# Two attention patterns and a soft mixture of experts: output stationaries read with a step, inputs packed in full tiles, another order

## The chip, the cores and the metric

The kernel runs on one core of one Trainium2 chip. Its time is device microseconds of one execution. Before the change three runs took 154.91 us at the median (154.8 to 155.06). The profile is of one further execution, which took 154.55 us.

## The reference, cut to what matters

```python
B, H, S, D = 4, 8, 768, 64                   # q, k, v: float32; is_retrieval = [1,0,1,0,0,0,1,0]
scores = q @ k.T / 8                         # for each batch and head
keep = causal & (retrieval[h] | (pos_k < 4) | (pos_q - pos_k < 64))
a = softmax(where(keep, scores, -1e9)); x = (a @ v) as (B*S, H*D) = (3072, 512)

logits = x @ phi                             # (3072, 32): 8 experts of 4 slots
d = exp(logits - max over tokens); d /= its sum over tokens
slot_in = d.T @ x                            # (32, 512)
slot_out[e] = relu(slot_in[e] @ w1[e]) @ w2[e]      # w1 (8,512,1024), w2 (8,1024,512)
c = softmax(logits over the 32 slots)
out = c @ slot_out                           # (3072, 512) float32
```

Every token of every batch takes part in the softmax over tokens, so nothing of the experts can start before the attention of the last batch has ended, and nothing of the output before the last expert.

## The kernel before, in words

**The order is written out.** The kernel builds its work as named operations (`Plan.op`), each with the engine it runs on, the operations it depends on, and the buffers it takes and gives back. The long string `ORDER` then says in which order they are emitted; `/A`, `/D` and `/P` put an operation on ACT, DVE or POOL. Each engine runs its own part of that string in order. A dependency becomes a wait in the engine's instruction stream, so what stands behind a waiting operation on the same engine waits too. SP issues the ten output stores, the flags and phi; POOL issues all other loads, since they turn float32 into bf16 on the way.

**Loading.** `slots` are twelve 8 KB-per-partition buffers. The twelve q, k and v loads (`Lq0` to `Lv3`, 768 KB in bf16 each, 96 partitions of 2 x 2048 elements) and the first twelve weight loads (`Lw0` to `Lw11`, 1 MB each) go through them. `Lw12` to `Lw15` go into memory that the attention has finished with: `Lw15` into the last batch's q and k (deps `qks[3]`). `Lw0` to `Lw7` are w1, `Lw8` to `Lw15` w2. The order of loads is Lq0 Lk0 Lv0 Lw0 Lq1 Lk1 Lv1 Lw1 Lw2 Lq2 Lk2 Lv2 Lw3 Lw4 Lw5 Lq3 Lk3 Lv3 Lw6 and so on.

**Attention.** A raw tensor is transposed on PE in four groups of 16 (`Tq0.0`, line 387: 64 columns of the raw tile at a time, 96 rows), into one PSUM bank (`TR`, two of them); each group is copied out by one instruction of 768 columns (`Eq0.0`, lines 232 and 234). For v a second transposition follows (`V2.p`, line 438, with `VB.p`). A pair p = 4b + n holds the heads n and n + 4 of batch b. For each pair there are five score groups `QK.p.0` to `QK.p.4` (line 406) into the PSUM buffers `SC` (two), their exponentials `EX.p.g` on ACT (line 474, 128x1024 each), their masks `MK.p.g` on DVE (line 418), six sums `PV.p.i` (line 522) into `PV` (one), the division `NM.p` on DVE (lines 533 and 535), and a transposition `XT.p` with its copy `XE.p` (line 547). `VF.p` (line 454) multiplies v with the head flags, mostly on POOL. `QX.b` and `EXX.b` do one score block of each pair of a batch together.

**Slots.** For each batch `LG.b` (line 561) makes the logits of its 768 tokens four times over, on 128 partitions, `EL.b` their exponentials `eTs` (128 partitions x 768 tokens), `DS.b` (line 618) the weighted sums of tokens, and `SA.b` adds them up. For the last batch these are `LGa.3`, `LTa`, `LTb`, `LGb.3`, `ET`, `DS.3`, `SA.3`, `EL.3`.

**The end.** After `SA.3`: `SI` and `SIE` bring the slot inputs into place (lines 673, 677), `H.e4.c` is the hidden layer of four experts, half c (line 687, 16 products each), `HR` its relu (lines 697, 699), `TH` and `HE` transpose it (line 708), `W2.e` the second layer of expert e (line 742), the last in two halves `W2.7.0` and `W2.7.1`, `SO` the scaling of the result (lines 757, 759). For the output, `EE.b` rearranges `eTs` into `expT` so that a stationary of 128 tokens is contiguous; `RW` (line 724) multiplies each of the 24 stationaries with a column for the softmax denominators, and `RWR` takes the reciprocals. The outputs are 24 products `OMf0` to `OMf23` (line 767), with their scaled copies `OEf` to SBUF (lines 772 and 774, on ACT and DVE) and ten stores `STf` (line 802). Product m = 4 gi + r makes the rows 512 gi + 4 p + r for the 128 partitions p, so a store of four r writes 8 KB in one run for each partition.

**Zeros.** `fill` puts products with zeros (line 330, `Z..`) on PE, each 128x512. `Z5`, eight of them, is a dependency of `W2.7`; `Z0`, `Z1` to `Z4` stand ahead of operations in the same way. The fills `Z60` to `Z67` depend on an early transposition only, and nothing depends on them.

The functions that the diff touches and what calls them, with the profile's line numbers:

## Time and profile before

| what | us |
|---|---|
| median of three runs | 154.91 |
| the profiled execution | 154.55 |
| its span, first to last instruction | 152.7 |
| PE busy | 133.0 |
| DVE busy | 113.4 |
| ACT busy | 107.5 |
| POOL busy | 33.5 |

The span lacks 1.85 us of the execution's own time. Times within the profile are counted from the span's start. A busy PE is not a PE at its peak: the products are pipelined, and a wait inside a stretch does not always show. PE's weight loads have a row of their own (PEld) and overlap the products. The profile's granted clock of PE is 1.00 at full and 0.50 at half speed; it is 0.969 over the span. A line of a group shows its count after an x, then busy microseconds and the mean nanoseconds of one. Lines 232, 234 and 239 are helpers (the copies on ACT and DVE, and the loads), so their rows are told apart by their tiles.

### The profile page before, as it was taken

How to read it: one execution, taken by the hardware profiler on the slowest of the kernel's cores; microseconds unless marked ns; L12 is line 12 of the kernel's file. 1: busy time of each engine (PE TensorE's matmuls, PEld its weight loads, DVE VectorE, ACT ScalarE, POOL GpSimd, SP SyncE). 2: the span in 40 equal slices, each digit the busy share in tenths (PEclk: the TensorE clock that was granted, in tenths of full speed). 3: DMA queues.
4: the chain of work that ended last, by engine and by line, in shares of the span. 5: the costliest groups of instructions: out<-in, count | busy, mean ns of one | idle time of the engine just before them, and what ended most of it. 6: DMA issues, size and time to landing. Idle time of an engine off the chain costs nothing.

```text
span 152.7 us, 5227 instructions
## 1 busy us (share of the span) xinstructions
PE 133.0 (87%) x2313; PEld 83.1 (54%) x2313; DVE 113.4 (74%) x257; ACT 107.5 (70%) x124; POOL 33.5 (22%) x51
## 2 busy tenths in 40 slices
PE   6999799999999999999989999998999689787100
PEld 2355456676677657677656676665673348232000
DVE  3955698999978799999998998999975322166900
ACT  3023699999999999999879999999917710266300
POOL 6910005750031060505520202405110000000000
PEclk9999999999999999999999999999999959999975
DMA  2999999999999999999999999999999992059995
GB/s 34 200 215 224 213 211 211 217 219 225 201 215 213 227 210 212 225 203 216 211 229 215 212 212 223 210 215 219 219 212 215 221 204 58 4 178 411 417 423 219
DMA packets 6950, 32.91 MB, mean 215 GB/s; under 512 B 1296, under 2 KB 1296, under 8 KB 4496
## 3 DMA queue, kind: packets, MB, share of 16 engines
q0 software_dynamic: 4800, 26.22, 83.8%
q1 hardware_dynamic: 2128, 6.37, 10.7%
q8 instruction: 18, 0.29, 0.7%
q14 instruction: 4, 0.03, 0.1%
HBM read 52.50 MB, written 6.29 MB: 385 GB/s over the span
## 4 chain that ended last, share of the span: by engine, by line
PE 59%; DVE 17%; DMA 8%; ACT 5%; issue 3%; POOL 2%; DVEq 0%; POOLq 0%; ACTq 0%
PE pv L522 13%; PE sc L406 13%; PE tr L387 9%; DMA slot<-in_v_dram 8%; DVE pt L418 5%; DVE slot L774 4%; PE sc L330 4%; PE tr L547 4%; PE tr L438 3%; DVE xv L535 3%; PE pv L742 3%; PE sc L561 3%; PE sc L687 3%; ACT pt L474 2%; DVE qk L234 2%
## 5 line engine op out<-in xcount | busy, mean ns | idle before, releaser
L474 ACT ACTIVATE pt<-sc 128x1024 bf16<-128x1024 f32 x80 | 77.6, 1026 | 4.8 <-PE sc L406 3.4
L418 DVE TENSOR_TENSOR pt<-pt,msk 128x512 bf16<-128x512 bf16 (+1 forms) x80 | 37.8, 503 | 1.2 <-ACT pt L474 1.2
L406 PE MATMUL sc<-qk 64*128 64x512 bf16 (+3 forms) x256 | 32.5, 309 | 0.0
L522 PEld LDWEIGHTS <-pt 128*128 128x128 bf16 x640 | 24.7, 97 | 9.1 <-issue 6.4
L522 PE MATMUL pv<-vx,pt 128*128 128x65 bf16 x352 | 27.9, 193 | 0.9 <-DVE xv L535 0.7
L387 PE MATMUL tr<-ident,slot 96*64 96x96 bf16 x768 | 24.1, 209 | 1.7 <-DMA slot<-in_v_dram 0.9
L454 POOL TENSOR_TENSOR vf<-vx,fm 128x528 bf16<-128x528 bf16 x14 | 15.5, 1112 | 44.8 <-DVE vx L234 43.0
L387 PEld LDWEIGHTS <-slot 96*64 96x64 bf16 x768 | 18.9, 110 | 10.6 <-issue 7.7
L522 PE MATMUL pv<-vf,pt 128*128 128x65 bf16 x288 | 22.7, 195 | 0.0
L330 PE MATMUL sc<-zero 128*128 128x512 bf16 x66 | 19.5, 429 | 1.2 <-DVE zero L321 1.2
L234 DVE COPY qk<-tr 128x768 bf16<-128x768 bf16 x28 | 14.9, 550 | 4.7 <-PE tr L387 4.5
L535 DVE TENSOR_TENSOR xv<-pv,rs 128x768 bf16<-128x768 f32 x16 | 15.3, 958 | 0.6
L406 PEld LDWEIGHTS <-qk 64*128 64x128 bf16 x256 | 9.2, 94 | 7.2 <-issue 1.6
L234 DVE COPY xT<-tr 128x768 bf16<-128x768 bf16 (+1 forms) x15 | 8.6, 570 | 5.2 <-PE tr L708 4.2
L239 POOL DMA_DIRECT2D slot<-in_moe_w_dram x12 | 6.8, 569 | 22.7 <-PE tr L387 16.3
L330 PEld LDWEIGHTS <-zero 128*128 128x128 bf16 x66 | 6.2, 108 | 9.1 <-issue 4.4
L232 ACT COPY qk<-tr 128x768 bf16<-128x768 bf16 x4 | 3.2, 797 | 10.8 <-PE tr L387 10.8
L234 DVE COPY xv<-tr 128x768 bf16<-128x768 bf16 x14 | 7.6, 552 | 1.9 <-PE tr L387 1.7
L547 PE MATMUL tr<-ident,xv 128*128 128x128 bf16 x96 | 8.1, 220 | 0.0
L438 PE MATMUL tr<-ident,xv 128*128 128x128 bf16 x96 | 8.0, 220 | 0.0
L234 DVE COPY vx<-tr 128x768 bf16<-128x768 bf16 x12 | 6.4, 551 | 1.0 <-PE tr L438 1.0
L547 PEld LDWEIGHTS <-xv 128*128 128x128 bf16 x96 | 5.6, 97 | 2.1 <-issue 1.8
(102 smaller groups left out, 135.3 us busy)
## 6 DMA issues: line engine op xcount, KB each, us to landing
slot<-in_moe_w_dram POOLq DMA_DIRECT2D x12, 1024.0 KB, 25.5
slot<-in_q_dram POOLq DMA_DIRECT2D x4, 768.0 KB, 18.4
slot<-in_k_dram POOLq DMA_DIRECT2D x4, 768.0 KB, 21.4
slot<-in_v_dram POOLq DMA_DIRECT2D x4, 768.0 KB, 23.7
out_dram<-slot SPq DMA_DIRECT2D x3, 1024.0 KB, 5.6
out_dram<-slot SPq DMA_DIRECT2D x5, 512.0 KB, 3.6
qk<-in_moe_w_dram POOLq DMA_DIRECT2D x2, 1024.0 KB, 18.3
vx<-in_moe_w_dram POOLq DMA_DIRECT2D x1, 1024.0 KB, 21.5
```

What stands on the lines that cost most here:

```text
L234: nc.vector.tensor_copy(dst, src)
L239: emit=lambda o: e.dma_start(dst(), src))
L330: nc.tensor.matmul(scb[buf.slot][:, 0, :], zero[:, 0:128], zero, start=True, stop=True)
L387: nc.tensor.transpose(t[64 * i:64 * (i + 1), :, s, :], rv[:, i, 8 * c + s, :], ident[0:96, 0:96])
L406: nc.tensor.matmul(scb[sc.slot][:, i, c:c + 128 * nb], kk, qq.rearrange("p b c -> p (b c)"), start=True, stop=True)
L418: e.tensor_tensor(pT[:, :, 0:w], pT[:, :, 0:w], mh[:, :, c:c + w], op=ALU.mult)
L438: nc.tensor.transpose(t[:, 128 * j:128 * (j + 1)], vT[:, 6 * n + j, :], ident)
L454: e.tensor_tensor(vfs[VFb[p].slot], vv, mm, op=ALU.mult)
L474: nc.scalar.activation(pTs[PTb[b, n].slot][:, :, 512 * g:512 * (g + 1)], scb[sc.slot], ACT.Exp, scale=scale)
L522: nc.tensor.matmul(pvb[:, h, 65 * i:65 * (i + 1)], lt, rhs, start=(j == 0), stop=(j == i))
L535: nc.vector.tensor_tensor(xo, pvw[:, :, :, 0:64], r.rearrange("p i (j o) -> p i j o", o=1).to_broadcast([P, 2, 6, 64]), op=ALU.mult)
L547: nc.tensor.transpose(t[:, 128 * i:128 * (i + 1)], xv[:, i, 128 * n:128 * (n + 1)], ident)
```

## The change

1. **Output stationaries.** For two thirds of the output (gi 2 to 5) the stationary is read out of `eTs` itself, every sixteenth column of the first 2048 tokens; only the last 1024 tokens are still rearranged into `expT` (gi 0 and 1), by two operations, `EE.2` (a third of a batch) and `EE.3`. The rows of an output tile gi of 2 to 5 are then 16 blocks of 8 x 4 neighbouring rows, and a store's pattern in DRAM has the dimensions 16, 8 and the run.
2. **Packing.** q, k and v of the batches 1 to 3, 864 rows in all, are laid one behind another into tiles of 128 rows: seven instead of nine. A tensor that crosses from a tile into the next is loaded in two parts. A tile's group of transposes handles all its rows, and one copy for each tensor in it follows (`Ek1.0.32/D` copies the rows from 32 on).
3. **Small work.** The second half of the slot tables goes to GpSimd, and `phi` to ACT. The tables `edist`, `phf` and `ri` lie in parts of `eTs` that are filled later.
4. **Zeros.** `Z5` is gone as a dependency. Ten fills `Z70` to `Z79` of two products each may stand anywhere behind `Z4`; in the new order `Z77` stands before `RW`, `Z73`, `Z71` and `Z75` before `W2.7.0`, the rest among the outputs.
5. **Order.** The whole string is another one. q of batch 3 is loaded ahead of `Lw3`. `EE.3` and `RW` stand ahead of `H`, the four `H` stand together, both `W2.7` ahead of `SO`.

```diff
+zero Lri Lq0 warm tables ident keypos flags Tq0.3 Lk0 Tq0.1 Lv0 Z0 hm3 Eq0.3/A hm0 Eq0.1/A Tq0.2 Tq0.0 Lw0
...
+LTa LGa.3 NM.15 XT.15 XE.15/D Z1 LTb LGb.3 Z2 ET DS.3 Z3 SA.3 EL.3 SI EE.3/D Z4 Lw15 Z77 RW SIE RC RWR H.0.1
+H.0.0 HR.0.1/D H.1.0 HR.0.0/A H.1.1 HR.1.0/A TH.0 HR.1.1/A TH.1 HE.0/D W2.0 W2.1 HE.1/D W2.2 W2.3 W2.4 W2.5
+W2.6 Z73 Z71 Z75 W2.7.0 W2.7.1 SO.0/D OMf0L SO.1/A OMf0R OMf1 OMf2 OEf0L OMf3 OEf0R OMf4 OEf1/A OMf5 STf0.0
...
-    expT = xv_mem[:, 6144:9216].rearrange("p (r c) -> p r c", r=4)
+    expT = sb.tile([P, 4, 256], BF16, name="expT")
...
+    tiles = [[(x, 0, 0, 0, 96)] for x in "qkv"]
+    row = 0
+    for b_, x_ in [(b_, x_) for b_ in range(1, B) for x_ in "qkv"]:
+        r0 = 0
+        while r0 < 96:
+            if row % 128 == 0:
+                tiles.append([])
+            n_ = min(96 - r0, 128 - row % 128)
+            tiles[-1].append((x_, b_, row % 128, r0, n_))
+            row, r0 = row + n_, r0 + n_
+    tbufs = [Buf("S8") for _ in tiles]
...
+    def emit_slot_tables(o):
+        nc.gpsimd.tensor_scalar(sum4, jrow[:, 0:NS], pc[:, 3:4], None, op0=ALU.is_equal)
+        nc.gpsimd.tensor_tensor(pc[:, 4:5], pc[:, 4:5], pc[:, 5:6], op=ALU.subtract)
...
                     for i in range(2):
                         nc.tensor.transpose(t[64 * i:64 * (i + 1), :, s, :], rv[:, i, 8 * c + s, :],
-                                            ident[0:96, 0:96])
+                                            ident[0:rows, 0:rows])
...
+            for x, b, p0, r0, n in parts:
+                tb = {"q": QTb, "k": KTb, "v": VTb}[x][b]
...
+                def emit_e(o, c=c, tr=tr, p0=p0, r0=r0, n=n, dst=dst):
+                    copy(o, dst()[:, r0 // 4:(r0 + n) // 4, 32 * c:32 * (c + 1)],
+                         tr_bf(tr.slot, 8 * rows).rearrange("p (x y) -> p x y", y=32)[:, p0 // 4:(p0 + n) // 4])
...
+    def evs(x, b, n=None):
+        return [o for r0, o in ev[x, b] if n is None or r0 < 24 * n + 24]
...
-    for b in range(B):
-        eto[b] = pl.op(f"EE.{b}", "ACT DVE", deps=[elo[b], dsp] + [xto[p] for p in range(12, 16)],
-                       emit=lambda o, b=b: emit_ee(o, b))
+    for b, x0 in ((2, 4), (3, 0)):
+        def emit_ee(o, b=b, x0=x0):
+            d_ = expT[:, :, 32 * (6 * b + x0 - 16):32 * (6 * b - 10)].rearrange("p r (x t a) -> p r x t a", t=4, a=8)
+            copy(o, d_, eTs[:, b, 128 * x0:768].rearrange("p (x a r t) -> p r x t a", a=8, r=4, t=4))
...
+    for i in range(10):
+        fill(f"Z7{i}", 2, [z4])
...
+    ef = eTs.rearrange("p b (k u) -> p u (b k)", u=16)
     def out_lhs(gi, r):
-        return expT[:, r, 128 * gi:128 * (gi + 1)]
+        return expT[:, r, 128 * gi:128 * (gi + 1)] if gi < 2 else ef[:, 4 * r + gi - 2, 0:128]
+    out_v = out.rearrange("(x t a r) d -> t x a r d", t=4, a=8, r=4)
+    out_n = out.rearrange("(g p r) d -> g p r d", p=128, r=4)
+    def out_dst(gi, r, c):
+        return out_n[4 + gi, :, r, c] if gi < 2 else out_v[gi - 2, 0:16, :, r, c]
...
-                z5 = [fill("Z5", 8, w2o[-1:] + [o_rwm])]
...
-            bf = Buf(["SC", "TR", "SC", "TR", "PV"][cyc % 5])
+            bf = Buf(["TR", "SC", "TR", "SC"][cyc % 4] if u < 12 else ["SC", "TR", "SC", "TR", "PV"][cyc % 5])
...
+              emit=lambda o, x=(gi, rr, cc): nc.sync.dma_start(out_dst(*x), ot_view(x[0])[:, x[1], x[2]]))
```

More of the change, by code (lines that the diff above doesn't have):

```diff
@@ L261, in w_view, with load_w @@
         return m.rearrange("p (a f) -> p a f", a=4 if i < NE else 8)
-    def load_w(i, deps=()):
+    def load_w(i, deps=(), rows=(128,), half=None):
         if i < NE:
@@ L348 @@
             for n in range(4)}
-    o_phi = pl.op("phi", "DVE", deps=o_ph, emit=lambda o: nc.vector.tensor_copy(
+    o_phi = pl.op("phi", "ACT", deps=o_ph, emit=lambda o: nc.scalar.copy(
         phi4.rearrange("p n (g s) -> p n g s", g=4),
@@ L419, in mask_emit @@
         return f
-    for b in range(B):
-        for x in "qkv":
-            transposes(x, b)
+    for g in range(len(tiles)):
+        transposes(g)
     tq0 = [o for o in pl.ops if o.name == "Tq0.3"]
```

271 lines of the change are left out of this document (143 added, 128 removed).

## The prediction

> **What bounds the kernel now.** I read the page's forty slices first, then windows, then the chain of waits from the end backwards, then the issues by tensor. The slices (3.8 us each, DMA busy in tenths, then GB/s written):
>
> ```profile
> span 152.7 us, 5227 instructions
> ...
> DMA  2999999999999999999999999999999992059995
> GB/s 34 200 215 224 213 211 211 217 219 225 201 215 213 227 210 212 225 203 216 211 229 215 212 212 223 210 215 219 219 212 215 221 204 58 4 178 411 417 423 219
> ```
>
> There are two long stretches with every DMA engine busy, and a hole between them. The first is the loading, the second the stores. So whatever the engines do, the time is: end of the loads, plus the hole, plus the stores. The last load (the second one into qk, which is Lw15) and the ten stores, from the answers on those tiles:
>
> ```profile
> L239 POOL DMA_DIRECT2D qk<-in_moe_w_dram x1: 536/536/536, 110.7 to 110.7; - x1
> ...
> DMA to landing us min/median/max: 17.9/17.9/17.9
> ```
> ```profile
> L802 SPq DMA_DIRECT2D out_dram<-slot x10: 332/332/547, 134.7 to 145.4; - x10
> ...
> DMA to landing us min/median/max: 2.5/3.9/6.2
> ```
> ```profile
> 76.00:113.00 37.00, 35.81 (x671) 24.24 (x669) 34.69 (x75) 33.57 (x38) 8.40 (x12) 1.00 1.04 217
> 117.30:129.60 12.30, 10.31 (x216) 6.56 (x216) 4.16 (x8) 3.60 (x5) 0.00 (x0) 0.86 0.80 167
> 134.70:151.60 16.90, 5.43 (x20) 1.63 (x17) 8.73 (x13) 6.10 (x10) 0.00 (x0) 0.85 0.93 372
> ```
>
> Lw15 is issued at 110.7 and lands 17.9 later, at 128.6. The first store is issued at 134.7, the last at 145.4, and that one lands 6.2 later, at 151.6; 1.1 us more end the span. The windows (columns: stretch, length, then busy time of PE, weight loads, DVE, ACT, POOL, the granted clock, DMA share, GB/s) show the stores at 0.93 of all engines over their 16.9 us, with DVE and ACT busy for only 8.7 and 6.1 of it: **the stores set their own length**, and it starts to run at the first store. So the question is when that store leaves. From the landing of Lw15 to it lie 6.1 us. The chain of waits there (start, length, what):
>
> ```profile
> 115.84 0.70 DVE msk L634
> ...
> 116.58 0.32 PE tr L673 x4
> ...
> 116.99 0.30 DVE msk L677
> ...
> 117.34 1.94 PE sc L687 x32
> ...
> 119.30 1.27 ACT msk L697 x2
> ...
> 120.62 0.72 PE tr L708 x8
> ...
> 121.36 0.69 DVE xT L234
> 122.05 0.67 DVE msk L699
> ...
> 122.76 1.90 PE sc L687 x16
> 124.66 0.73 PE tr L724 x24
> 125.39 1.37 PE pv L742 x24
> 126.76 0.64 PE tr L708 x8
> 127.40 2.30 PE pv L742 x80
> 129.70 1.83 PE sc L330 x8
> 131.53 0.36 PE pv L742 x8
> ...
> 131.91 0.48 ACT msk L757
> ...
> 132.44 0.40 PE pv L742 x8
> ...
> 133.62 0.50 PE sc L767 x2
> ...
> 134.20 0.49 DVE slot L774
> ```
>
> Read it as: slot sums (SA.3), SI, SIE, the hidden layer H (L687), its relu HR (L697, L699), its transpose TH and copy HE, the slot weights' row sums RW (L724), W2 (L742), eight zeros Z5, the last expert W2.7, its scaling SO, the first output row. All of it is PE's order, not data: W2.7.0 needs Lw15, there at 128.6, but starts at 131.53. **The hole has 2.9 us that no transfer asks for** ahead of W2.7.0, and 3.2 us behind it.
>
> **The change part by part.** The terms move the first store; the stores' length follows.
>
> *The end of attention.* The rows for the packed transposes and evictions:
>
> ```profile
> L387 PE MATMUL tr<-ident,slot 96*64 96x96 bf16 x768 | 24.1, 209 | 1.7 <-DMA slot<-in_v_dram 0.9 <-DVE qk L234 0.5 <-DVE msk L305 0.2
> ...
> L234 DVE COPY qk<-tr 128x768 bf16<-128x768 bf16 x28 | 14.9, 550 | 4.7 <-PE tr L387 4.5
> ...
> L232 ACT COPY qk<-tr 128x768 bf16<-128x768 bf16 x4 | 3.2, 797 | 10.8 <-PE tr L387 10.8
> ...
> L234 DVE COPY elg<-tr 128x192 bf16<-128x192 bf16 x3 | 0.8, 252 | 0.2 <-PE tr L583 0.2
> ```
>
> The nine later tensors, 864 rows, become seven tiles, so 28 groups of 16 transposes replace 36. A group costs 24.1/48 = 0.50 (all 48 groups are in that row). Eight fewer save 4.0 us of PE if a group of 128 columns costs what one of 96 does, and lose 0.8 if it costs by the column (28 x 0.67 against 36 x 0.50); I take 2 saved, between them, spread over 70 us. But the evictions grow from 36 to 52: sixteen times a group is cut in two. From 550 ns for 768 columns and 252 for 192, a column costs 0.52 ns and an instruction 0.15 us, so 16 cuts cost at most 2.5 us in all; by the pace of copies that follow one another it is less, some 1.2. By the written order ACT keeps three of its nine full copies (797 ns each) inside the attention and gets two small pieces, EG.1 and phi; what it drops goes to DVE, which in turn drops phi, one VF and the second half of the slot tables. In the window 76 to 113 DVE has 34.69 of 37.00 and ACT 33.57: both are near full, DVE the fuller. After 76 us my count of the two orders gives ACT 1.4 us less (EL.1 is earlier, VB.13 goes to DVE, EG.1 comes) and DVE about nothing (three full evictions less, four small ones, VB.11 and VB.13, EE.2 more, VF.13 less). So the end of attention moves between -1.4 (ACT's share) and +0.6 (the cuts not covered); I take -0.5, since DVE is the fuller.
>
> The slot tables on GpSimd and four more load issues (split tensors; some 0.66 each, the row of the k loads below) cost nothing: POOL is busy 8.4 of 37 us, and the loads behind them are issued long before their turn (Lw15 17.9 ahead). Without that cover they would be 2.6 us and the small ops. Lw14 now stands ahead of VF.15 on POOL, and PV.15 waits for VF.15; but Lw14's last condition, DS.2, stands before QK.15 in the new order, so I cost it at nothing, and at what DS.2 is late if it slips.
>
> *From SA.3 to H.* EE.3 and RW now stand ahead of H on their engines: DVE does SA.3, EE.3, SIE, and PE does RW before H.0.1, so H waits for both. The rows, from the timeline:
>
> ```profile
> 117.20 1.69 DVE L234 COPY xv<-eT 128x768 bf16<-128x768 bf16 x2
> ...
> 120.45 1.62 ACT L232 COPY xv<-eT 128x768 bf16<-128x768 bf16 x1
> ...
> 120.61 0.57 PEld L708 LDWEIGHTS <-msk 128*128 128x128 bf16 x8 [1.00 <-ACT msk L697]
> ...
> 124.59 0.71 PEld L724 LDWEIGHTS <-xv 128*128 128x128 bf16 x24 [0.84 <-issue]
> ```
>
> EE.3 on DVE is 1.69/2 = 0.85: from 116.54 to 117.39. RW took 0.73 with 24 contiguous loads, 0.71/24 = 30 ns each. Sixteen of them now step 16 elements. No row shows that step; the transposes of L708 load with a step of 8 and take 0.57/8 = 71 ns. Bounds: nothing (RW 0.73), or double the excess of L708 (+1.3, RW 2.0). I take L708's 71 for each, the nearest row: +0.66, RW 1.39, to 118.8. So H starts at 118.8 instead of 117.34: **+1.46**. In the 24 output products the same loads are covered by the stores. The Trainium skill (SBUF — State Buffer, Door 1: The DMA port swizzle) calls steps of up to 8 bf16 elements free and lets longer ones pay at each new 16-byte line. The trace does not agree on the first, 71 ns against 30, and has no longer step; if each load reads 128 lines at either step, as the rule has it, the two cost the same, which is the 71 taken here.
>
> *H to the last W2.* Before, 12.2 us (117.34 to 129.70 less RW 0.73 is 11.6 of own work): H.1.0 waits for HR.1.1, which waits behind HE.0 on DVE, and runs at half clock (16 products 1.90, where 32 took 1.94). After, the four H stand together: 4 x 0.97 = 3.88, to 122.7. TH.0 0.64 to 123.3; meanwhile HR.1.0 and HR.1.1 on ACT, 1.27, from 122.7 to 124.1 with two hand-overs; TH.1 0.64 to 124.75; seven W2 at 2.30/5 = 0.46 each, 3.22, to 128.0. EE.2's 1.62 on ACT, and EE.0 and EE.1, are gone from here. The zeros: Z5's eight took 1.83; "no forced zeros" is only half so, since Z73, Z71 and Z75 stand at the same place, 6 x 0.23 = 1.37, to 129.35. With -0.5 from attention **W2.7.0 starts at 128.85**, against 131.53. Lw15 forbids anything before 128.6, so a faster attention brings 0.25 more and then nothing. That landing should not move by more than 1 us either way: the same bytes in almost the same order, behind a queue that the slices show full throughout.
>
> *W2.7.0 to the first store.* Before 3.18: W2.7.1 waits for SO.0, then SO.1, then two products. After, both halves run first (0.76), SO.0 on DVE and SO.1 on ACT together (0.48), two half products in one bank (0.4), the two evictions together (0.49), and some 0.17 of hand-overs: 2.3. First store at 131.15, **3.56 earlier** than 134.71.
>
> *The stores.* Same ten, same bytes, same run of one to four rows for each partition, in the same order; evictions keep their pace and their banks differ little. I take 16.9 unchanged, which is a choice: two thirds of the bytes now go to 16 blocks of 8 partitions, and no row shows that form (rival 2).
>
> Sum: profiled time 154.55 - 3.56 = 151.0. The three runs have a median 0.36 above the profiled one, so **151.3**.
>
> **The rivals.** *1, the hole closes less, for attention is late.* A tile is transposed only when both tensors in it have landed. Tq3 was ready with q3; now it needs k3, and every QK and PV stands behind it on PE (Tv1 waits for q2 in the same way):
>
> ```profile
> L239 POOL DMA_DIRECT2D slot<-in_k_dram x4: 641/663/702, 3.1 to 45.5; - x4
> ...
> DMA to landing us min/median/max: 9.0/21.4/30.8
> ```
>
> The last k lands at 45.5 + 30.8 = 76.3 and PE, in order, stands there if it comes sooner; DVE at 34.69 of 37 cannot win it back. With +1.5 instead of -0.5, W2.7.0 is at 130.85: 153.3, faster still. For it: both engines nearly full. Against: two SC buffers keep ACT fed for 2 us.
>
> *2, the stores get slower, and so the kernel.* If the 16 engines take a block each, eight neighbouring partitions, pairs of them may read the same part of SBUF while another part is idle. At half rate the 4.2 MB, at 372 GB/s 11.3 us, take 11.3 more: 162.6. It decides from the point where 11.3 us become 14.9, that is at 0.76 of today's rate. For: the outer dimension really changes from 128 to 16. Against: 16 is still one for each engine, and every run of bytes stays as long. The Trainium skill has a rule that would do it: DMA: Bandwidth & Descriptors (Why a DMA increments its semaphore by 16 and not by 1) shares a transfer out along the slowest dimension of its patterns, and SBUF — State Buffer (Door 1) puts partitions 32 apart on one port. No run here shows it yet.
>
> *3, the clock.* H and W2 at half clock, as at 122.76 (0.86 granted over 117.3 to 129.6). Four H would cost 3.9 more, W2.7.0 at 132.75: 155.2, slower. For: fewer forced zeros. Against: PE's gaps are now 0.5 and 0.7 us where it had 1.4 and more, and Z4, Z77 fill the first.
>
> **How the numbers follow.** Forecast 0.56 (150.4 to 152.4: Lw15's floor, RW's two bounds, attention's two bounds); rival 1 0.16; rival 2 0.16; rival 3 0.12, half of it within 0.2% as it may hold for part of the stretch. 0.2%, 0.3 us, is about what a measurement of this kernel tells from no change. Faster 0.56 + 0.16 = 0.72, same 0.06, slower 0.22. The range, 149.8 to 155.2, takes in rivals 1 and 3 and a landing of Lw15 1 us sooner, and leaves out rival 2.
>
> **What would show it.** W2.7.0 within 0.4 us of Lw15's landing, and that landing at 128.6 give or take 0.7. RW at 1.4 before H, H's 64 products in 3.9 at full clock. First store 2.3 behind W2.7.0. Stores from first issue to last landing 16.9; anything over 18 is rival 2, in the strided ones alone. The last NM 0.5 sooner; PE waiting at Tq3 for k3 near 76 is rival 1. I am wrong if the stores lengthen, or if H starts later than 119.5.

## The result, and the profile after

The changed kernel took **155.99 us** at the median of twenty runs (155.25 to 158.41), the kernel before 154.62 beside it (153.22 to 156.15). The ratio is **1.0114 (95% interval 1.0086 to 1.0142)**: it is slower by 1.1%, where 151.3 was forecast. Four further runs gave 1.0141 (1.0052 to 1.0230). Some executions of either kernel are some per cent slower at a lower granted clock; the ratios leave them out, and the profile read here is not one of them: 156.44 us long, span 154.5.

The page of it, the lines that answer to the first ones of before:

```profile
span 154.5 us, 5010 instructions
...
DMA  1999999999999999999999999999999980199992
GB/s 22 209 216 219 221 206 212 222 217 214 204 215 212 214 226 214 210 223 207 211 227 214 218 216 212 218 212 218 216 214 214 221 172 19 46 389 346 331 405 112
```

The hole between loads and stores has become shorter, but behind it one slice of before is missing: the stores, 411 to 423 GB/s before once they ran, now pass through 346 and 331 first. The last load, the ten stores, and the windows of the end of the attention, of the way from RW to W2, and of the stores (columns as before):

```profile
L241 POOL DMA_DIRECT2D qk<-in_moe_w_dram x2: 536/565/594, 91.2 to 111.3; - x2
...
DMA to landing us min/median/max: 17.6/20.3/23.1
```
```profile
L859 SPq DMA_DIRECT2D out_dram<-slot x10: 332/485/881, 133.9 to 145.9; - x10
...
DMA to landing us min/median/max: 2.5/3.9/7.9
```
```profile
76.00:113.00 37.00, 34.60 (x632) 22.99 (x630) 35.67 (x77) 34.10 (x40) 9.01 (x12) 1.00 1.04 217
...
119.46:129.50 10.04, 9.25 (x218) 6.82 (x214) 2.63 (x6) 1.96 (x3) 0.00 (x0) 1.00 0.78 163
133.90:153.40 19.50, 9.41 (x31) 3.84 (x29) 6.39 (x9) 8.00 (x14) 0.00 (x0) 0.79 0.89 323
```

Lw15 lands at 111.3 + 17.6 = 128.9, as forecast. The first store leaves at 133.9, 0.8 sooner than before instead of 3.6, and the stores last 19.55 us instead of 16.93 (133.89 to 153.44; before 134.71 to 151.64). The chain of waits between:

```profile
119.46 1.17 PE tr L774 x24
120.63 3.60 PE sc L727 x64
124.31 1.28 ACT msk L737 x2
125.63 0.71 PE tr L748 x8
126.34 3.17 PE pv L789 x112
129.51 1.40 PE sc L356 x6
130.91 0.58 PE pv L789 x16
131.51 0.50 DVE msk L806
132.03 0.48 ACT msk L804
132.87 1.13 ACT slot L820 x2
134.02 0.76 DVE slot L822
```

Line by line it is RW (L774), H in one piece (L727), HR, TH.1, seven W2 (L789), six zeros (L356), W2.7, SO.0, SO.1, the first evictions. H to W2.7.0 is as short as forecast: 130.91 - 120.63 = 10.28, against 14.19 before. But it starts late, because the last normalisation (NM.15) does. From the rows of the reciprocal that opens each normalisation, the last one before and after:

```profile
111.92 0.23 DVE L533 RECIPROCAL rs<-pv 128x12 f32<-128x12 f32 x1 [0.24 <-PE pv L522]
```
```profile
113.86 0.23 DVE L569 RECIPROCAL rs<-pv 128x12 f32<-128x12 f32 x1 [0.36 <-PE pv L558]
```

So three things make the result: the attention ends **1.94 us later**, the way from there to the first store is 2.76 shorter (133.89 - 113.86 = 20.03, against 134.71 - 111.92 = 22.79), the stores take **2.62 longer**. That is +1.8, the difference of the spans.

### The profile page after: what moved, and what is told of

It is laid out like the page before. It is cut to its first block, busy times and chain, and to the rows that moved or that the text cites. A ratio compares the mean times of both kernels' runs of the same rounds, so it can differ in the third digit from the quotient of the medians.

```text
span 155.8 us, 5002 instructions
## 1 busy us (share of the span) xinstructions
PE 133.9 (86%) x2189; PEld 84.8 (54%) x2197; DVE 112.2 (72%) x264; ACT 103.4 (66%) x125; POOL 38.2 (25%) x61
## 4 chain that ended last, share of the span: by engine, by line
PE 63%; DVE 13%; DMA 8%; ACT 5%; issue 3%; POOL 2%; POOLq 0%; ACTq 0%
PE pv L558 14%; PE sc L443 14%; PE tr L413 11%; DMA slot<-in_v_dram 8%; DVE pt L455 6%; PE sc L356 5%; ACT slot L820 4%; PE sc L597 3%; PE tr L474 3%; PE tr L583 3%; DVE xv L571 2%; PE pv L789 2%; PE sc L727 2%; DVE vx L236 2%; PE tr L654 1%
## 5 line engine op out<-in xcount | busy, mean ns | idle before, releaser
L455 DVE TENSOR_TENSOR pt<-pt,msk 128x512 bf16<-128x512 bf16 (+1 forms) x80 | 38.8, 515 | 0.2
L490 POOL TENSOR_TENSOR vf<-vx,fm 128x528 bf16<-128x528 bf16 x15 | 16.9, 1132 | 41.8 <-DVE vx L236 24.4
L413 PE MATMUL tr<-ident,slot 128*64 128x128 bf16 (+1 forms) x640 | 23.7, 221 | 2.4 <-DVE xv L571 1.9
L356 PE MATMUL sc<-zero 128*128 128x512 bf16 x71 | 21.6, 426 | 3.9 <-ACT slot L820 1.3
L413 PEld LDWEIGHTS <-slot 128*64 128x64 bf16 (+1 forms) x640 | 18.3, 112 | 10.2 <-issue 6.2
L236 DVE COPY qk<-tr 128x768 bf16<-128x768 bf16 (+2 forms) x35 | 15.3, 459 | 6.2 <-PE tr L413 6.1
L356 PEld LDWEIGHTS <-zero 128*128 128x128 bf16 x78 | 7.3, 107 | 13.1 <-issue 7.7
L236 DVE COPY xv<-tr 128x768 bf16<-128x768 bf16 (+2 forms) x22 | 9.3, 430 | 2.9 <-PE tr L413 2.6
L234 ACT COPY qk<-tr 128x768 bf16<-128x768 bf16 x5 | 3.9, 804 | 10.5 <-PE tr L413 10.5
L236 DVE COPY vx<-tr 128x768 bf16<-128x768 bf16 x15 | 8.3, 553 | 1.1 <-PE tr L474 0.9
```

Of the source, the lines that this page charges most:

```text
L236: nc.vector.tensor_copy(dst, src)
L356: nc.tensor.matmul(scb[buf.slot][:, 0, :], zero[:, 0:128], zero, start=True, stop=True)
L413: nc.tensor.transpose(t[64 * i:64 * (i + 1), :, s, :], rv[:, i, 8 * c + s, :], ident[0:rows, 0:rows])
L455: e.tensor_tensor(pT[:, :, 0:w], pT[:, :, 0:w], mh[:, :, c:c + w], op=ALU.mult)
L490: e.tensor_tensor(vfs[VFb[p].slot], vv, mm, op=ALU.mult)
```

## The experiments

Theories at the start: S, the strided stores are slow; A, the packed attention is late; and their rivals. Below, "last NM" is the start of that reciprocal (the expectations count from the product behind it, 0.27 us later), "pair 1 to last NM" the time to it from the same instruction of pair 1, and "stores" the time from the first store's issue to the last landing.

| kernel | pair 1 to last NM | last NM | first store | stores | ratio to before, interval |
|---|---|---|---|---|---|
| before | 78.26 | 111.92 | 134.71 | 16.93 | 1 |
| changed | 81.61 | 113.86 | 133.89 | 19.55 | 1.0114 (1.0086 to 1.0142) |
| store_plain | 81.63 | 114.06 | 134.09 | 16.73 | 0.9950 (0.9918 to 0.9983) |
| store_gaps | 81.62 | 113.20 | 133.22 | 16.74 | 0.9985 (0.9941 to 1.0030) |
| store_128k | 81.62 | 113.82 | 133.85 | 18.64 | 1.0142 (1.0073 to 1.0212) |
| store_192k | 81.61 | 114.03 | 134.05 | 21.14 | 1.0217 (1.0092 to 1.0342) |
| store_halves | 81.61 | 115.16 | 135.18 | 28.54 | 1.0803 (1.0741 to 1.0865) |
| tq1_later | 81.62 | 114.87 | 134.90 | 19.31 | 1.0155 (1.0090 to 1.0221) |
| unpacked | 79.54 | 117.62 | 137.58 | 19.48 | 1.0376 (1.0265 to 1.0488) |
| unpacked2 | 80.60 | 114.38 | 134.35 | 19.29 | 1.0217 (1.0128 to 1.0305) |
| v1_alone | 83.45 | 115.65 | 135.67 | 19.21 | 1.0273 (1.0185 to 1.0361) |
| q2_first | 81.59 | 113.15 | 133.18 | 18.70 | 1.0114 (1.0071 to 1.0157) |
| ev_dve | 80.84 | 113.23 | 133.25 | 19.34 | 1.0061 (1.0014 to 1.0109) |
| vf_out | 79.37 | 111.46 | 131.90 | 18.93 | 1.0000 (0.9962 to 1.0038) |
| vf_moved | 79.17 | 113.01 | 133.03 | 19.37 | 1.0046 (1.0015 to 1.0077) |
| no_zeros | 81.62 | 114.02 | 132.54 | 20.78 | 1.0132 (1.0062 to 1.0202) |
| early_hidden | 78.26 | 112.08 | 133.52 | 17.75 | 0.9951 (0.9916 to 0.9986) |
| hidden_fill | 78.26 | 112.07 | 133.16 | 16.93 | 0.9938 (0.9914 to 0.9962) |
| **hidden_split** | 78.25 | 111.96 | 132.31 | 16.95 | **0.9882 (0.9854 to 0.9911)** |

Last NM moves by 2 us between profiles of kernels whose attention is the same (113.20 to 115.16 in the store kernels). All of that arises before pair 1 is normalised (31.58 to 33.55 in them), where PE waits for the load of k1. From pair 1 on, these kernels take 81.61 to 81.63, so what an edit does to the attention behind pair 1 is read from that column. The stores vary too: the same 16 blocks, 256 KB apart, take 18.70 to 19.55 in the profiles where nothing behind the last NM was changed.

### The stores

The changed kernel itself, for this profile and as the pair of the others:

> The changed kernel once more, for a profile that stands beside the next three on the same chip. Theory S (stores): the four output tiles whose DRAM pattern is 16 blocks of 8 rows drain slower; the last 4.19 MB take some 12.4 us from the landing of the tenth megabyte-half before them to the end, where the kernel before took 9.9. Theory P (packing): PE stops at Tq1.0 until the first part of k1 has landed (26.8 us), where the kernel before went on, and the last NM comes 1.5 to 3.5 us later than 112.2. Both are expected here; ratio to before 1.01.

**store_plain** sends the strided rows to plain places:

```diff
-        return out_n[4 + gi, :, r, c] if gi < 2 else out_v[gi - 2, 0:16, :, r, c]
+        return out_n[4 + gi, :, r, c] if gi < 2 else out_n[gi - 2, :, r, c]
```

> The changed kernel with the stores of gi 2 to 5 written to 128 neighbouring row groups of 4 instead of 16 blocks of 8, so the rows of the output stand in another order; everything else is the same. Theory S: 2.4 us less than the changed kernel, first store to last landing 16.9 instead of 19.3, some 153.5 us. If instead the stores are late because the evictions feed them worse, 0 to 0.3 less.

The stores are back at 16.73 and the kernel is faster than before. The strided loads of the products are still there, so it is the stores' form alone that costs: S holds. **store_128k** and **store_gaps** ask what in the form:

```diff
+    out_h = out[0:2048].rearrange("(o x h a r) d -> o h x a r d", o=2, x=16, h=2, a=8, r=4)   # store_128k
+    out_h = out[0:2048].rearrange("(o p h r) d -> o h p r d", o=2, p=128, h=2, r=4)           # store_gaps
```

> The changed kernel with the 16 strided rows of output sent to other places: each store still writes 16 blocks of 8 partitions (64 KB each), but the blocks lie 128 KB apart instead of 256 KB. Rows of the output stand in another order, nothing else differs. The changed kernel took 19.55 us from the first store's issue to the last landing, with plain stores 16.73. Theory P (the distance of 256 KB between blocks written at the same time costs): nearer to plain, 17 to 18 us, time about 154.3. Theory B (that a store is cut in 16 separate blocks at all costs): 19.5 us again, time about 156.5.

> The changed kernel with each of the later stores as 128 rows of 8 KB that lie 16 KB apart: no two descriptors touch each other in memory, but there is one even distance and no blocks. Rows of the output stand in another order, nothing else differs. Theory P (large even distances between blocks written at once) and theory B (16 blocks): about 16.8 us from first issue to last landing, as with plain stores, time about 153.7. A third theory G (a store needs its neighbours in memory side by side): 19 us or more, time 156 or more.

Rows with gaps cost nothing (G falls). Blocks cost, 1.9 us at half the distance. That is less than the 2.8 of the changed kernel's profile, but the other profiles with 256 KB go down to 2.0 (18.70), and the kernel's time did not fall (1.0142), so these runs do not show that the distance matters: between P and B. Two more kernels: **store_halves** issues each strided store as two of 64 partitions, **store_192k** writes three of the four groups at 192 KB.

> The changed kernel with each strided store issued as two stores of 64 partitions (8 blocks each) instead of one of 128 (16 blocks). Plain stores took 16.7 us from first issue to last landing, 16 blocks 128 KB apart 18.6, 16 blocks 256 KB apart 19.55. Theory P (16 engines that start together at the same offset of their blocks get in each other's way): 17.5 to 18.7, since only 8 blocks are written at once and two engines share each. Rival (the number of separate blocks or the order of the engines has nothing to do with it): 19.3 to 19.8.

> The changed kernel with three of its four strided groups of rows written as 16 blocks of 64 KB that lie 192 KB apart, the fourth group plainly. Rows of the output stand in another order, nothing else differs. From first issue to last landing, plain stores took 16.7 us, 16 blocks 128 KB apart 18.6, 256 KB apart 19.55. Theory P (engines that write at one offset of blocks an even power of two apart get in each other's way): 192 KB is no power of two, 16.7 to 17.3. Theory B (one block of eight neighbouring partitions for each engine costs wherever it is written): three quarters of the 128 KB case's excess or more, 18.1 to 18.8.

Both theories fall in the form I gave them. The halves took 28.5 us. Windows of the changed kernel, of store_plain and of store_halves (the last three numbers are granted clock, DMA share, GB/s):

```profile
140.00:143.00 3.00, 2.02 (x7) 0.82 (x6) 1.41 (x2) 2.11 (x4) 0.00 (x0) 0.81 1.00 328
143.00:146.00 3.00, 3.00 (x10) 1.00 (x8) 0.75 (x1) 1.32 (x3) 0.00 (x0) 0.63 1.06 328
146.00:150.00 4.00, 0.35 (x2) 0.00 (x0) 0.00 (x0) 0.00 (x0) 0.00 (x0) 0.83 0.99 389
```
```profile
143.00:146.00 3.00, 2.22 (x9) 0.67 (x7) 0.75 (x1) 1.48 (x3) 0.00 (x0) 1.00 1.02 426
```
```profile
150.00:155.00 5.00, 0.00 (x0) 0.00 (x0) 0.00 (x0) 0.00 (x0) 0.00 (x0) 0.50 0.51 215
```

A store of 8 blocks keeps half of the engines busy (0.51), at half the rate, as it would if **the outermost dimension were dealt out to the engines, one block to each**. The Trainium skill states this (DMA: Bandwidth & Descriptors, Why a DMA increments its semaphore by 16 and not by 1: a transfer takes the largest number of engines up to 16 that divides its slowest dimensions), and the trace agrees. No run here tells the 8 blocks from the 64 partitions, since the halves have both. With 16 blocks all engines are busy, but their packets take longer. In the records of the stores' packets 8 KB took 307 to 345 ns with plain stores; in the changed kernel those that began between 144 and 145 us took 614 ns on average, the longest 912, and by 150 us they are at 311 again, still in blocks. So a block form is not slow as such. It is slow for 2 us where it begins (packets of 4 KB that began between 140 and 141 took 261 ns, where 160 is usual) and for 4 us where its run length changes (143 to 147), and its engines then end at different times (16 packets in flight at 151 us, 10 at 151.5, 3 at 152.25). In store_192k, which goes over from blocks to plain rows for the last store, a second slow stretch stands at 148 to 151. Which part of the path the engines get in each other's way on **stays open**: 128, 256 and 192 KB cost 1.9, 2.0 to 2.8 and 4.4 us, so it isn't the distance alone. The pairs of engines of rival 2, which would meet only while the engines keep step, are not excluded either: no run changes which partitions a block holds.

### The end of the attention

**tq1_later** moved the first two packed transposes of batch 1 (`Tq1.0`, `Tq1.1`) behind `QK.2.3`, for ACT and PE stand there until k1 has landed (26.8 us):

> The changed kernel with Tq1.0 and Tq1.1 behind QK.1.2, QK.2.1 and QK.2.3 in PE's order, nothing else. Theory P: the stop at 24.5 to 26.9 is gone or shorter, the clock stays at 1.00, EX.2 starts 1 to 2 us sooner and the last NM 1 to 2 sooner: 154 to 155 us. Rival D (DVE is the bound of the attention, by the sixteen cut copies and the copies that came from ACT): the time is made up before the end, under 0.5 us less.

A miss: the stall moved on. The last exponential of pair 1 began at 25.67 instead of 27.89, but the gap then stood between the exponentials at 28.86 and 32.46, and the last NM came later still, all of it by pair 1 (from there it takes 81.62, as without the edit).

**unpacked** put tiles of 96 rows and before's order in front of the changed end.

> The attention of the kernel before (q, k and v in tiles of 96 rows, its order, its engines for the copies), with the slot tables, the strided stationaries, the stores and the tail order of the changed kernel. Theory P and rival D together say what packing and the new attention order cost: last NM back at 112.2, the tail 2.7 us shorter than before from SA.3 to the first store, stores 2.4 longer: 154.3 us, about the kernel before. If the attention is not what is late, it stays at 155.5 to 156.

It came out latest of all but one, by a flaw of my edit: the slot tables stood so early on GpSimd that it waited for VectorE's part of them with Lv0 and the first weights behind it. Lw15 landed at 132.0. It says nothing on the packing. **unpacked2** has the slot tables behind `VF.2`:

```diff
+    tiles += [[(x_, b_, 0, 0, 96)] for b_ in range(1, B) for x_ in "qkv"]
 ... PV.13.5 EE.2/D QK.14.4 ...
```

> Tiles of 96 rows and the order of the attention as in the kernel before, everything behind the last normalisation (strided stationaries, strided stores, no forced zeros, the order of the end) as in the changed kernel; the slot tables on GpSimd stand behind the third mask copy, where that engine is idle. Theory A (the packing and its order cost the 1.9 us by which the last normalisation came later): last normalisation 112.2 to 112.8 (before 112.19, changed 114.13), first store about 132, and with the slow stores of 19.5 us a span of about 151.8, time about 154. Rival (the slot tables or the copies of the end make the attention late whatever the tiles): last normalisation 113.5 or later, span 153.5 or more, time 156.

Another miss, and the one that told most. Up to pair 12 its normalisations are those of before (100.58 against 100.36), then the last is 2.46 late, without any packed tile. What differs in the order there is one copy, EE.2, that I had put on VectorE. It is not the whole of the 2.46: pair 13 is 1.39 late, and the rest comes while the granted clock is 0.50, from 108.7 to 112.1. VectorE and GpSimd at that place:

```profile
103.72 1.24 DVE L446 TENSOR_TENSOR pt<-pt,msk 128x512 bf16<-128x512 bf16 x1 [0.19 <-ACT pt L501]
104.88 1.25 DVE L234 COPY expT<-eT 128x256 bf16<-128x256 bf16 x1
```
```profile
103.61 2.27 POOL L481 TENSOR_TENSOR vf<-vx,fm 128x528 bf16<-128x528 bf16 x2 [5.45 <-DVE vx L234]
```

The same copy takes 0.39 in the changed kernel. Here it takes 1.25 and ends when the second GpSimd operation (VF) ends; the mask product ahead of it takes 1.24 instead of 0.42 beside the first. **A VectorE instruction that works from SBUF to SBUF stands still while GpSimd computes.** The Trainium skill says so (SBUF — State Buffer, Who interferes with whom: an instruction of VectorE with both inputs in SBUF, or a copy in its two-port mode, and a GpSimd instruction that reads SBUF hold each other off, and the one issued first keeps the shared ports for all of its length). The trace agrees but for one product that began first and was held all the same (last section). Normalisations, which read PSUM, keep their 0.96 beside the same VF in the traces read here. Now the changed kernel, GpSimd and VectorE:

```profile
92.98 1.06 POOL L490 TENSOR_TENSOR vf<-vx,fm 128x528 bf16<-128x528 bf16 x1 [1.24 <-DVE vx L236]
...
95.39 2.11 POOL L490 TENSOR_TENSOR vf<-vx,fm 128x528 bf16<-128x528 bf16 x2
106.33 0.59 POOL L241 DMA_DIRECT2D xv<-in_moe_w_dram  x1 [8.82 <-PE tr L654]
106.94 1.08 POOL L490 TENSOR_TENSOR vf<-vx,fm 128x528 bf16<-128x528 bf16 x1
```
```profile
95.84 1.95 DVE L455 TENSOR_TENSOR pt<-pt,msk 128x512 bf16<-128x512 bf16 x1
...
106.34 2.44 DVE L455 TENSOR_TENSOR pt<-pt,msk 128x512 bf16<-128x512 bf16 x3
```

One product held for 1.95 by two VF in a row, and three that should take 1.2 take 2.44 beside VF.15, which came then because it stands behind Lw14 on GpSimd and Lw14 waited for DS.2 until 106.33. **vf_out** tests it by leaving these four VF out:

```diff
-                e.tensor_tensor(vfs[VFb[p].slot], vv, mm, op=ALU.mult)
+                if p < 12:
+                    e.tensor_tensor(vfs[VFb[p].slot], vv, mm, op=ALU.mult)
```

> The changed kernel without the masked copies of v for the last four pairs (VF.12 to VF.15, on GpSimd at 93.0, 95.4, 96.4 and 106.9 us): they are left out, so the sinks of the streaming heads use old values there. In the changed kernel three mask products on VectorE that meet these four run 0.75, 1.95 and 1.64 us instead of 0.42, 3.1 us more in all, 2.8 of it behind pair 12. Theory H (VectorE is held up while GpSimd computes, and that sets the end of the attention): those products take 0.42, the last normalisation comes 1.2 to 2.8 us sooner (114.1 to about 112), time about 154.5. Rival R (the long products are only waits that ACT's scores would have caused anyway): the last normalisation stays within 0.4 of 114.1, time 156.3.

H holds, in full: the last NM at 111.46 (vf_out's row, in the same view as above):

```profile
111.46 0.23 DVE L570 RECIPROCAL rs<-pv 128x12 f32<-128x12 f32 x1 [0.36 <-PE pv L559]
```

That is 2.40 sooner (2.24 of it behind pair 1), and 0.46 sooner than in the kernel before. The time is that of before although the stores still take 18.93. **vf_moved** keeps the work and changes only when it runs (`VF.7` stands later as well):

```diff
-"VB": 2, "VF": 3,
+"VB": 2, "VF": 2,
 ... PV.11.5 VF.13/P ... PV.12.5 VF.14/P ... PV.13.5 VF.15/P ...
```

> The changed kernel with all its work, but two buffers instead of three for the masked copies of v, so that each waits for the pair before the last, and the copies of pairs 13 to 15 placed right behind the last product of pairs 11 to 13: they should run while VectorE normalises (1.2 us, reads PSUM, was never seen longer beside GpSimd). Theory H (where the copies fall decides): the mask products behind pair 12 keep 0.42 to 0.55, the last normalisation at 111.7 to 112.5 as without the copies (111.7; the changed kernel 114.1), first store about 132, time 154.3. Rival (the copies cost VectorE the same wherever they fall): last normalisation above 113.5, time above 156.

Behind pair 1 all of it came. Only VF.12 still holds a product (0.81); VF.13 to VF.15 run under normalisations, the last three pairs take 12.19 us instead of 12.94, and from pair 1 to the last NM it is 79.17, as without the copies (79.37) and 2.44 less than in the changed kernel. That the last NM is still at 113.01 comes from pair 1, 1.6 us late in this profile. Its row in the changed kernel and in vf_moved, then a window of each of vf_moved and store_halves:

```profile
32.25 0.23 DVE L569 RECIPROCAL rs<-pv 128x12 f32<-128x12 f32 x1
```
```profile
33.84 0.23 DVE L569 RECIPROCAL rs<-pv 128x12 f32<-128x12 f32 x1 [0.23 <-PE pv L558]
```
```profile
28.00:32.00 4.00, 3.78 (x46) 2.22 (x47) 2.08 (x6) 2.41 (x3) 1.50 (x3) 0.57 1.10 222
```
```profile
28.00:32.00 4.00, 3.87 (x55) 2.37 (x55) 2.31 (x6) 2.13 (x3) 3.46 (x6) 0.75 1.08 219
```

PE waited 1.82 us for k1 there, and behind that the granted clock was 0.50 for 3.4 us. It is not the two buffers: they hold back `VF.3` alone there (33.83 instead of 29.50), and it belongs to pair 3, which comes as long after pair 1 as in the changed kernel. And store_halves, which has three buffers, shows the same (a wait of 1.77, clock 0.50, pair 1 at 33.55). In time vf_moved is 1.0046 where the changed kernel is 1.0114; its profile is of one of its longer executions (155.41, median 154.64).

The other loss is at pair 5, where the rows of ACT in the changed kernel are these:

```profile
47.12 1.94 ACT L510 ACTIVATE pt<-sc 128x1024 bf16<-128x1024 f32 x2 [0.33 <-PE sc L443]
50.67 0.37 ACT L234 COPY xv<-tr 128x256 bf16<-128x256 bf16 x1 [1.61 <-DVE qk L236]
50.94 1.95 ACT L510 ACTIVATE pt<-sc 128x1024 bf16<-128x1024 f32 x2
```

I read this first as the wait of the packed tile of v1 and q2 for q2 (rival 1 of the prediction). **v1_alone** gives v1's last rows a tile of their own, **q2_first** issues q2 ahead of Lw2:

```diff
-            if row % 128 == 0:
+            if row % 128 == 0 or (x_, b_) == ("q", 2):                       # v1_alone
...
-... Lw2 MK.0.3 ... Lq2 ...                                                   # q2_first
+... Lq2 Lw2 MK.0.3 ...
```

> The changed kernel, but the last 32 rows of v1 have a tile of their own and q2 starts the next tile alone with 96 rows, its transposes 1 to 3 us later in the order: the transposes of v1 no longer wait for the landing of q2 (45.9 us). Theory W (this wait is what the attention loses): the gap of ACT from 48.04 to 50.94 is gone, the normalisation of pair 5 (61.12) comes 1.5 to 2 us sooner and the last one at about 112.3 instead of 114.13, time about 155. Rival D (VectorE sets the end of the attention and early stalls are made up for by then): pair 5 sooner, but the last normalisation between 113.7 and 114.5, time within 0.4 of the changed kernel (156.5).

> The changed kernel with one load moved: q2 is issued ahead of the third weight load (2 MB), so it should land near 41 us instead of 46.0, before the packed tile of v1 and q2 is transposed. No instruction is added. Theory W (the wait of that tile for q2 costs the attention about 2 us at pair 5 and they are not made up): ACT's gap from 48.04 to 50.94 shrinks below 1 us, pair 5 is normalised about 1.5 to 2 us sooner than 61.1, and the last pair 1 to 2 us sooner than 114.1, time about 155. Rival D (VectorE and its holds behind pair 12 set the end): pair 5 sooner, the last pair within 0.4 of 114.1, time 156.3.

In v1_alone the gap at pair 5 went (the exponential of 50.94 came at 49.14), but the transposes and copies of one tile more put pair 5's normalisation back from 60.85 to 62.60, and that 1.75 reached the end undiminished (1.79): a delay there isn't made up. In q2_first q2 landed at 41.06 instead of 46.01 and the wait stayed as it was, 1.61, with the same releaser; from pair 1 to the last NM it takes 81.59, as without the edit. So W falls, and the row names the cause itself: ACT's copy of v1's piece waits for *VectorE's copy of q2's piece*, out of the same PSUM bank. **ev_dve** gives both to VectorE (`Ev1.0.64/A` becomes `Ev1.0.64/D`):

> The changed kernel with one copy moved from ACT to VectorE: the second piece of v1 (chunk 0) out of the packed tile that it shares with q2. In the changed kernel ACT stands 1.6 us, from 49.06 to 50.67, until VectorE has copied q2's piece out of the same bank; exponentials queue behind it. Theory T (two engines that read one tile of PSUM are put one behind the other, so a packed tile whose pieces go to two engines stops one of them): the wait is gone, the exponential of 50.94 comes at 49.3 or sooner, pair 5 is normalised 0.8 to 1.6 us sooner than 61.1. At the end, if VectorE's holds by GpSimd behind pair 12 set it, the last normalisation stays within 0.5 of 114.1 and the time at 156.3; if not, it comes 0.8 to 1.6 us sooner and the time is about 155.2. Rival Q (ACT waits for q2's data, not for the bank): the exponential stays at 50.5 or later.

T holds. The exponential comes at 49.68, and counted from pair 1 the normalisation of pair 5 comes 0.78 sooner (27.82 instead of 28.60) and the last one 0.78 sooner (80.84 instead of 81.61). It is at the small end of what I expected, since PE's scores now come 0.48 late, and the end moved although GpSimd holds VectorE there: the last 20 us are a chain, not a limit that absorbs what comes before.

### The hole between loads and stores

**no_zeros** moved the three fills between W2.6 and W2.7.0 behind `Z76`:

> The changed kernel with the six zero products between W2.6 and the last expert moved behind the output's evictions, where nothing waits for them. Theory Z (the last expert now waits for TensorE's own order, not for its weights, landed at 128.9): the first store 1.2 to 1.4 us sooner than 133.9, time about 155.3. Rival L (the last weights set it anyway): first store within 0.3. Rival C (without them the clock falls for the output's products): the product of the first rows takes twice as long and the first store comes no sooner.

The first store came 1.35 sooner, as Z had it, but the time stayed: I had put the zeros among the output's products, where eight of them now take 1.89 us at 133.47, in the chain. For the total it decides nothing. Rival C did not come: the granted clock stayed at 1.00 through these products.

**early_hidden** takes the kernel before, with its contiguous stationaries and stores, and reorders its end alone:

```diff
-SIE EE.0/A Z4 H.0.1 H.0.0 HR.0.1/A H.1.1 HR.0.0/A EE.1/D TH.0 EE.2/A EE.3/D HE.0/D HR.1.1/D H.1.0 RW ...
-... W2.6 Z5 W2.7.0 SO.0/A W2.7.1 OMf0L SO.1/D
+SIE EE.0/A Z4 H.0.1 H.0.0 EE.1/D EE.2/D H.1.1 H.1.0 HR.0.1/D HR.0.0/A EE.3/D HR.1.1/A TH.0 HR.1.0/A HE.0/D TH.1
+W2.0 W2.1 HE.1/D W2.2 ... W2.6 RC RW RWR Z5 W2.7.0 W2.7.1 SO.0/D OMf0L SO.1/A      (Z5: 6 zeros, not 8)
```

> The kernel before with only its end in another order: the hidden layer's four parts one behind the other, its first part not behind the row sums, the row sums between W2.6 and the last expert, EE.2 moved from ACT to VectorE, both halves of the last expert ahead of the scaling, six zeros instead of eight. Stationaries, tiles and stores stay contiguous as before. If the hole of before was TensorE's order and nothing else: last normalisation 112.2, W2.7.0 at the landing of its weights, 128.6 to 128.9 (before 131.5), first store 3.0 behind it at 131.7 (before 134.7), stores 16.9: 3.0 us faster, time 151.0 to 151.8. If the gain of the changed kernel's end needs the strided stationaries (no copies EE.0, EE.1): first store after 133, time 153.5 or more.

It is faster than before by 0.5%, a quarter of what I expected. PE's rows there, and the clock in a window of early_hidden and of the next kernel:

```profile
129.74 0.62 PE L741 MATMUL pv<-qk,xT 128*32 128x256 bf16 x16 [1.34 <-DMA qk<-in_moe_w_dram]
...
132.38 0.58 PE L766 MATMUL sc<-msk,xv 128*128 128x512 bf16 x1 [0.56 <-ACT slot L771]
```
```profile
130.00:134.00 4.00, 2.61 (x22) 0.92 (x11) 1.48 (x3) 1.42 (x3) 0.00 (x0) 0.65 0.00 0
```
```profile
130.00:134.00 4.00, 2.62 (x22) 1.08 (x15) 1.63 (x3) 1.78 (x4) 0.00 (x0) 1.00 0.00 0
```

The last expert did wait for its weights, with PE idle for 1.34 us, and behind that the clock was down (0.65; 0.50 from 132 to 135). The landing itself was at 129.70, 1.1 later than before. In the packet records the load's last engine is two packets behind the others; why isn't known, and the next two kernels have it too (landings at 129.65 and 129.59). **hidden_fill** has ten zeros there; **hidden_split** also puts the right half of output row 0 into a bank of its own:

```diff
-z5 = [fill("Z5", 6, ...)]
+z5 = [fill("Z5", 10, ...)]
+            if nm == "R":                      # hidden_split only
+                bf = Buf("TR"); bank = lambda bf=bf: trb[bf.slot]
```

> As early_hidden, with ten zeros instead of six ahead of the last expert, so that TensorE is busy until 129.2 (it ended at 128.3 and stood for 1.3 us). Theory C (the clock that fell to 0.50 in that wait held the first rows back): granted clock 1.00 from 130 to 140, output products 0.21 us instead of 0.43, first store 131.8 to 132.6, stores 16.9, time 151.5 to 152.3. Rival (the first store waits for something else): clock up and first store still 133 or later, time 153.

> As hidden_fill, with the second half of the first row of output in a bank of its own, so that the two evictions of that row on ACT and VectorE are not one behind the other. Theory S (two engines that touch one tile of PSUM are put one behind the other, which made the way from the last expert to the first store 3.0 instead of 2.3): first store 0.4 to 0.6 sooner than in hidden_fill. Rival (the evictions are bound by the products): no difference.

The clock came back in full (second window) and the stores with it, 16.93 instead of 17.75. But the first store moved by 0.36 only, and the medians are equal, 153.27 and 153.26 (from two chips; the ratios' intervals overlap): early_hidden's profile is of its longest execution, 154.47. So the clock goes with 0.8 us of the stores in that one execution, but C, by which it held the first rows back, loses to its rival (clock up, first store still after 133), and the zeros do not change the usual time. S holds with more than it promised, 0.85 us. The chains of hidden_fill and of hidden_split behind W2.7:

```profile
129.69 0.65 PE pv L741 x16
130.36 0.49 DVE msk L758
130.88 0.48 ACT msk L756
131.71 0.48 ACT slot L771
132.24 0.39 PE sc L766
132.65 0.49 DVE slot L773
```
```profile
129.79 0.58 PE pv L741 x16
130.39 0.49 DVE msk L758
130.94 0.35 issue
131.28 0.47 ACT slot L771
131.80 0.39 PE sc L766
```

In the first each half eviction waits for the other and for the next product of the same bank; in the second the two are independent and the first store leaves 2.52 behind W2.7.0. **hidden_split is the version that beats both kernels**: 152.46 us, 0.9882 of the kernel before, and it has nothing of the change but an order of the end like its own; the second tile for row 0 is new.

## Why the prediction was wrong

By its own steps, in order:

- **"The end of attention ... I take -0.5"** failed: +1.94. Up to pair 1 the changed kernel is 1.41 sooner than before, in spite of its wait for k1; from there to the last NM it takes 81.61 instead of 78.26, 3.35 longer. Of that the four VF behind pair 11 are 2.24 (vf_out) to 2.44 (vf_moved), and the two copies of v1 and q2 on two engines 0.78 (ev_dve). If these add up, which no run tests, 0.1 to 0.3 is left. That vf_out ends 0.46 sooner than before, near the -0.5, is chance: 1.58 sooner at pair 1, 1.11 longer behind it. What failed is that the step prices work on GpSimd by POOL's own load (8.4 of 37 us, "cost nothing") and not by what VectorE does meanwhile. From 93 us on VF held mask products for 3.1 us, in the kernel before for 1.3: there one of the last two VF ran beside a normalisation, and the new order put all four beside masks. The step named the place ("Lw14 now stands ahead of VF.15 on POOL") and priced only DS.2's lateness, not whom VF.15 would meet.
- **"SA.3 to H ... +1.46"** held: from 117.75 to 120.63 it is 2.88, before 1.50, so +1.38. The sixteen loads with a step of 16 took 1.07, 67 ns each, against the 71 taken; the two steps cost the same.
- **"H to the last W2"** held: 10.28 against 10.55, H's 64 products 3.60 against 3.88, at full clock.
- **"The two evictions together (0.49)", 2.3 in all** failed: 2.98. SO.0 and SO.1 read one PSUM tile, and so do the two halves of the first row, and each pair ran one behind the other. For the row hidden_split shows that the shared tile is the reason; for SO.0 and SO.1, whose halves are two banks of that tile, it is not shown.
- **"Stores 16.9, which is a choice"** failed: 19.55. It is rival 2 at a smaller size. I had its decision point at 0.76 of the rate; the 11.3 us of strided bytes became about 13.9, 0.81 (13.1, 0.86, by the shortest of the profiles), so alone it would have left the kernel faster. And the pairs of engines that it blamed were not shown: the blocks reach full rate later.

The sum: first store forecast at 131.15; attention +2.44, RW -0.08, H to W2.7.0 -0.27, behind it +0.68 make 133.92 (measured 133.89). The stores add 2.62, so 5.4 in the span, 149.1 forecast, 154.5 measured. One slip in the working decides nothing: 117.34 to 129.70 is 12.36 us, not 12.2.

Of the rivals, 1 had the right sign and nearly the right size (+1.5), by the wrong mechanism: what cost at the tile of v1 and q2 was its two copies on two engines, not the landing of q2, and between 70 and 80 us PE waits for no load at the tile of q3. Its mechanism does show at the first packed tile, of q1 and k1, which it did not name: PE waits there for k1, 1.73 us in the changed kernel. Rival 3, the clock, did not come: 1.00 from 119.46 to 129.50. It came in one execution of early_hidden, behind a wait of 1.34 us that six zeros did not fill.

## What to carry to other kernels

Before work goes to GpSimd or moves in its queue, lay its instructions over VectorE's SBUF-to-SBUF ones in the timeline: a short instruction that takes a long one's time there is a hold, and it belongs under work that reads PSUM. Give two engines two tiles of PSUM when they are meant to work side by side. Compare profiles from a point behind the first loads, not from the start: here 2 us of difference lay ahead of it. A store's outermost dimension decides how many DMA engines it uses (8 blocks kept half of them busy); a rearrangement that is saved on chip and moved into the store's pattern has to be timed as a store.

## What the runs showed that was not expected

- VectorE's mask product of 0.42 us took up to 1.95 beside two GpSimd operations in a row: it did not get in between them. A product recorded as begun 0.27 us *before* a GpSimd operation (106.67 and 106.94) was held by it all the same, for 1.2 us; others, begun 0.2 us before one (65.48, 74.92), kept their 0.41.
- A store of 64 partitions in 8 blocks used 8 of 16 DMA engines (share 0.51, 215 GB/s). One of 16 blocks used all, at 309 ns for 8 KB in its steady part and up to 912 ns in the first microseconds of its 8 KB runs.
- 1.34 us without a product stood ahead of a clock of 0.50 on PE for the first rows of output, in one execution. Waits for k1 of 1.77 and 1.82 us stood ahead of a clock of 0.50 in store_halves and vf_moved; one of 1.73 in the changed kernel left it at 1.00.
